# A new order of the ramp, with 60 matmuls on a zero tile, in a fused attention and gated-MLP kernel

## The chip, the cores and the metric

The kernel runs on one core of one Trainium2 chip. The metric is the device time of one execution in microseconds. Times are compared as medians of several runs. A profile comes from one further execution of the program.

## What is computed

The input is `q`, `k` and `v` with 4 batches, 8 heads, 768 positions and 64 columns. Heads 0, 2 and 6 ("retrieval") attend to all earlier positions; the other five ("streaming") attend to the first 4 positions and to a window of 64. The result of attention, 3072 rows of 512, goes through a gated layer of width 2048.

```
scores = scale * q @ k.T
mask   = causal                              # retrieval heads
mask   = causal & (is_sink | in_win)         # streaming heads, n_sink 4, window 64
a      = exp(scores - max) ; a = a / sum(a)
x      = a @ v                               # -> (B*S, H*D) = (3072, 512)
h      = x @ w_in                            # (3072, 2048)
g      = h * sigmoid(beta * h)
out    = g @ w_out                           # (3072, 512), float32
```

## The kernel before

The work is cut in eight chunks (a batch and a half of its 768 positions) and each chunk in four units (a pair of heads), 32 units in all. Each unit goes through the same steps:

- keys and queries arrive by DMA in float32 (tile `s`), are cast to bf16 (`qkb`, L246), transposed on TensorE (L322) and copied to the tiles `KT` and `QTD` (L330, L333). From unit 12 on, DMAs that cast and transpose do this instead (L282, L294, L297);
- values are cast to `VX` (L251); copies with the first four positions in front, for the streaming heads, go to `VO` (L259, L260) and `KO` (L312);
- scores go to a pair of PSUM banks (`sp`, L451). In the units up to 7 the masks are added first by a matmul with an identity (L422); later, and for unit 5, VectorE multiplies the exponentials by a mask (L478);
- ScalarE takes the exponential into `es` (L460), TensorE multiplies by the values into `po` (L520; odd units of the first eight use a bank of the pool `mm`), and VectorE divides (L529, L533) into `x`;
- `x` is transposed, on TensorE and by a copy in the first two chunks (L558, L567), by DMA later (L548), into `xT`.

The gated layer is cut in two kinds of steps: G1 makes 128 of the 2048 columns for a chunk (four matmuls of 128x384, L588), with a tanh on ScalarE (L593) and the gate on VectorE (L596); G2 adds four of sixteen products of 128x512 into an output tile (L641), which ScalarE scales (L645) and a DMA stores (L647).

The order of instructions on each engine is the order in which the program issues them; nothing reorders them afterwards. Up to unit 7 a string of words, `RAMP`, writes this order by hand: `ck`/`cq` cast keys or queries of a unit, `tk`/`tq` transpose them, `kk`/`kq` copy the transposes out (the last letter names the engine: v VectorE, a ScalarE, g GpSimd), `ko` copies sink keys, `ad`, `qk`, `ex` and `ma` are mask product, scores, exponential and mask multiplication of one score tile, `pv` is a third of a unit's value products, `no` its division, `xx` and `cx` the transposes of x and their copy, `lv`, `lq`, `wi`, `wo`, `ro` issue loads (a `g` at `lv` or `lq` lets a memset on GpSimd hold the load until that place in GpSimd's order), `cv`, `vo` and `on` prepare values, `mm` and `mA` issue a G1 step into a bank of one pool or the other, and `mb` a G2 step. `hm` and `hf` are the two halves of one G1 step. After that, `PLAN` does the same with one line per unit: `V` scores, `p` a sixth of the value products, `a`/`A` G1, `b` G2, `T` and `X` transposes.

Loads of keys, queries and values and the stores go through the queue of SP, two of the first loads through that of ScalarE, weights and later rows through that of GpSimd. `later` puts off some small VectorE and GpSimd steps by a planned delay.

Before the ramp, eight matmuls of 128x512 on a tile of zeros are issued (`idle(8, ps_m, "mm")`, L167, L168).

Of the kernel before, what the change touches and what calls it, by code (L numbers as in the profile page):

```python
# [10 lines left out]
F32 = mybir.dt.float32  # L11
# [7 lines left out]
def kernel(  # L19
# [13 lines left out]
    nc = tc.nc  # L33
# [348 lines left out]
    def steps_QK(u):  # L382
# [117 lines left out]
        some = 3 if len(tiles) == 3 else 2  # L500
        return [visit(range(i, min(i + some, len(tiles)))) for i in range(0, len(tiles), some)]

    def steps_PV(u):
        b, h2, p = units[u]
        s = st_u.setdefault(u, {})

        def head(hh, qi, last):
            def go():
                for f in s["masks"] + chunk_values[u // NPAIR] if u >= 8 else []:
                    f()  # L510
                if "po" not in s:
                    if u < 8 and u % 2:
                        po = ps_m.tile([128, 512], F32, name="mm")
                        s["po"] = po[:, 0:HT * 2 * (D + 1)].rearrange("p (t h d) -> p t h d", t=HT, h=2)
                    else:
                        s["po"] = ps_o.tile([128, HT, 2, D + 1], F32, name="po")
                po = s["po"]
                lst = s["blocks"][hh][qi]
                for j, (e, val) in enumerate(lst):
                    nc.tensor.matmul(po[:, qi, hh, :], e, val, start=(j == 0), stop=(j == len(lst) - 1))  # L520
# [142 lines left out]
    h = FO // 2  # L663
# [21 lines left out]
    def do(word):  # L685
# [7 lines left out]
        elif what in ("kk", "kq"):  # L693
            copy_qk(n, what[1], copies[eng])
        elif what == "ko":
            sinks_of(n)
        elif what in ("ad", "qk", "ex", "ma"):
            if n not in visits:
                visits[n] = steps_QK(n)
            step((0 if what in ("ex", "ma") else 170, lambda: visits[n][what](i)))  # L700
        elif what == "cv":
            cast_v(n, i, copies[eng])
        elif what == "vo":
            sink_values(n)
        elif what == "pv":
            pv = products.setdefault(n, [])
            if not pv:
                pv.extend(steps_PV(n))
            run(pv[:2])
            del pv[:2]  # L710
        elif what == "no":
            normalize(n)
        elif what == "xd":
            x_by_dma(n)
        elif what == "xx":
            run(steps_X(n))
        elif what == "cx":
            copy_x(n, copies[eng])
        elif what == "on":
            ones_v(engines[eng], n)  # L720
        elif what == "ne":
            negatives([(0, 1, 2), (3, 4)][n])
        elif what == "be":
            step((100, beta_go))
        elif what == "lv":
            load_v(n, held=eng == "g", tiles=[i])
        elif what == "lq":
            load_qk(n, i, held=eng == "g")
        elif what == "wi":
            load_w_in(n)  # L730
        elif what == "wo":
            load_w_out(n)
        elif what == "rq":
            rows_queries()
        elif what == "rk":
            rows_keys()
        elif what == "ro":
            if n not in more_rows:
                more_rows[n] = load_rows(n)
            more_rows[n].pop(0)()  # L740
        elif what in ("dk", "dq"):
            transposes_dma(n, what[1])
        elif what == "ml":
            late[n].pop(0)()
        elif what == "tt":
            run(steps_T(n))
        elif what == "hm":
            opened.append(done[0])
            done[0] += 1
            step(halves[0](opened[-1], 0))  # L750
        elif what == "hf":
            step(halves[0](opened.pop(0), 1))
        else:
            feed({"mm": "a", "mA": "A", "mb": "b"}[what])

    def feed(x):
# [24 lines left out]
        qk7.0 ad7.1 pv5 pv5 ex7.0 lv3.2 qk7.1 pv5 no5 ml1 wo1 ex7.1 pv6 pv6 wo2 mm pv7 rq  # L781
        pv7 pv7 no7 wo3 pv6 no6 rk cq8g xx2 ro3 cx2a mA mA ck8g xx3 cx3a mm mA
        mm mA mm mm mA mm mm mm mA mm ro3 mm mm mA mm mm mm ro3
        mA mm ro3 mA mm ro3 mm mm ro3 mA mA mb mb tt8 mb mb mb
    """
    words = RAMP.split()
    on_vector = {int(w[2]) for w in words if w.startswith("ma")}
    for word in words:
        do(word)

    PLAN = """
        ro3 ro3 ck9v b cq9a dk3 b cv2.1v cv2.0v vo2 T ro3 cv2.2v V cq11v a ro3 ro3 ro3 ck11a ro4 a b
        ck10a a dq3 a p cq10v a V p T p p p V p
        b T b p p p p p V p
        A b A a V ro4 p V a p p ro4 p p p
        ro4 V b p p p b p p ro4 p V b
        b p p p p X V p p a ro4 a ro4
        b A ro4 a a p V p ro4 p p ro4 b ro4 a a A ro4 A b b b dk4 A V a p dq4 p b A b
        p p p p p V p a a
        p p A p V p p p  # L800
        a a b b p p p p p p V a A A
        a b p p p p V p p
        b b a V p p p p p b a p
        b A A a a A p a A A a p b a p A p p p A A V b b b A
        p V p p p p p
        a A a b b p p p V p p b p a A
        a p A b p b p b A p b a p b p V A a
        V a p p b p p b V p p A
        b p p p p V p p
        A a b V b b a a p p b p A p a p a a A A p b V a b A b b  # L810
        p p p p V p p
        a A V b p A A p p p V p p a A
        a p b V b p p p p p
        V b a p a p p V A p A b b p p A A a
        p b V a p p p p A a p
        b a A p a p a a b a A p p A b a p b a p
        b A X a A b A
    """.strip().split("\n")
    TAIL = "aaAaA"

# [79 lines left out]
```

## Time and profile before

| what | value |
|---|---|
| median of 3 runs | 229.58 us (228.45 to 230.4) |
| the profiled execution's own time | 231.07 us |
| its span, first to last instruction | 229.1 us |
| TensorE (PE) busy | 223.1 us, 97% |
| ScalarE (ACT), VectorE (DVE), GpSimd (POOL) busy | 154.3, 141.8, 87.6 us |

The span is the time between the first and the last instruction of the program; the execution's own time is 1.97 us longer. The profile models the ends of matmuls, which are pipelined, so that a row of several matmuls gives their rate better than the duration of one. A row of the order of time reads: start, length, engine, line, operation, output<-inputs, shape, count, and in brackets the idle time before it with what ended it. A name with q (SPq) is the queue of an engine, in which DMAs are issued.

### The profile page before, as it was taken

How to read it: one execution, taken by the hardware profiler on the slowest of the kernel's cores; microseconds unless marked ns; L12 is line 12 of the kernel's file. 1: busy time of each engine (PE TensorE's matmuls, PEld its weight loads, DVE VectorE, ACT ScalarE, POOL GpSimd, SP SyncE). 2: the span in 40 equal slices, each digit the busy share in tenths (PEclk: the TensorE clock that was granted, in tenths of full speed). 3: DMA queues.
4: the chain of work that ended last, by engine and by line, in shares of the span. 5: the costliest groups of instructions: out<-in, count | busy, mean ns of one | idle time of the engine just before them, and what ended most of it. 6: DMA issues, size and time to landing. Idle time of an engine off the chain costs nothing.

```text
span 229.1 us, 5018 instructions
## 1 busy us (share of the span) xinstructions
PE 223.1 (97%) x1907; PEld 127.4 (56%) x1907; DVE 141.8 (62%) x342; ACT 154.3 (67%) x254; POOL 87.6 (38%) x143
## 2 busy tenths in 40 slices
PE   7899999999999999999999999999999999999994
PEld 2456666654565665555654565455654656455553
DVE  4458988875286588536952588546963779028600
ACT  2567988864868799438944697759876878138621
POOL 5373991219636269535028038940560000000000
PEclk9999999999999999999999999999999999999999
DMA  6999999999999999969778969496983130111012
GB/s 202 262 297 247 215 197 203 232 193 161 196 142 97 181 164 156 122 173 156 111 149 109 158 132 173 86 163 93 194 70 83 47 83 0 49 46 46 0 49 92
DMA packets 95383, 31.66 MB, mean 138 GB/s; under 512 B 81776, under 2 KB 92416, under 8 KB 95360
## 3 DMA queue, kind: packets, MB, share of 16 engines
q1 hardware_dynamic: 58880, 22.82, 48.6%
q0 software_dynamic: 35904, 8.13, 39.8%
q10 hardware_dynamic: 576, 0.40, 0.5%
q8 instruction: 15, 0.25, 0.4%
q14 instruction: 8, 0.07, 0.1%
HBM read 27.27 MB, written 6.29 MB: 146 GB/s over the span
## 4 chain that ended last, share of the span: by engine, by line
PE 94%; DMA 2%; ACT 1%; SPq 0%; issue 0%; ACTq 0%
PE mm L641 35%; PE mm L588 25%; PE sp L588 12%; PE sp L451 8%; PE po L520 7%; PE mm L322 2%; DMA s<-in_k_dram 2%; PE sp L422 2%; PE mm L626 2%; PE mm L558 1%; PE mm L520 1%; PE mm L451 1%; ACT qkb L246 1%; SPq L119 0%; ACT es L460 0%; ACT KT L330 0%
## 5 line engine op out<-in xcount | busy, mean ns | idle before, releaser
L641 PE MATMUL mm<-w_out_sb,gT 128*128 128x512 bf16 x368 | 85.9, 379 | 0.0
L460 ACT ACTIVATE es<-sp 128x768 bf16<-128x768 f32 (+2 forms) x72 | 56.6, 837 | 21.4 <-PE sp L451 21.2
L588 PE MATMUL mm<-xT,w_in_sb 128*128 128x384 bf16 x348 | 64.6, 326 | 0.0
L588 PEld LDWEIGHTS <-w_in_sb 128*128 128x128 bf16 x512 | 47.8, 98 | 29.8 <-issue 0.2
L593 ACT ACTIVATE th<-mm,beta_h 128x384 f32<-128x384 f32 x87 | 49.7, 587 | 5.7 <-PE mm L588 0.9
L641 PEld LDWEIGHTS <-gT 128*128 128x128 bf16 x368 | 33.4, 98 | 36.0 <-issue 1.5
L596 DVE SCALAR_TENSOR_TENSOR gT<-th,mm 128x384 bf16<-128x384 f32 x87 | 46.7, 551 | 6.7 <-ACT th L593 3.2
L282 POOL DMA_DIRECT2D s<-in_q_dram x30 | 22.4, 763 | 26.3 <-DMA QTD<-s 19.8
L588 PE MATMUL sp<-xT,w_in_sb 128*128 128x384 bf16 x164 | 32.3, 326 | 0.0
L645 ACT ACTIVATE osb<-mm 128x512 f32<-128x512 f32 x23 | 13.9, 603 | 25.5 <-PE mm L641 25.2
L520 PEld LDWEIGHTS <-es 128*128 128x128 bf16 x472 | 23.8, 99 | 12.8 <-issue 1.5
L596 DVE SCALAR_TENSOR_TENSOR gT<-th,sp 128x384 bf16<-128x384 f32 x41 | 22.3, 552 | 5.6 <-ACT th L593 3.7
L282 POOL DMA_DIRECT2D s<-in_k_dram x30 | 22.4, 760 | 8.5 <-DMA w_out_sb<-in_moe_w_out_dram 5.8
L593 ACT ACTIVATE th<-sp,beta_h 128x384 f32<-128x384 f32 x41 | 23.7, 585 | 2.3 <-PE sp L588 0.2
L520 PE MATMUL po<-VX,es 128*128 128x65 bf16 x360 | 25.2, 195 | 0.0
L251 POOL CAST VX<-vs 128x512 bf16<-128x512 f32 x16 | 10.1, 632 | 36.4 <-DMA vs<-in_v_dram 30.2
L529 DVE RECIPROCAL rec<-po 128x6 f32<-128x6 f32 x28 | 5.4, 193 | 29.1 <-PE po L520 29.1
L451 PE MATMUL sp<-QTD,KT 64*128 64x128 bf16 (+2 forms) x258 | 20.1, 249 | 0.6 <-ACT QTD L333 0.4
L478 DVE TENSOR_TENSOR es<-es,Mh 128x768 bf16<-128x768 bf16 (+1 forms) x26 | 15.5, 626 | 5.0 <-ACT es L460 4.4
L533 DVE TENSOR_TENSOR x<-po,rec 128x384 bf16<-128x384 f32 x28 | 15.6, 557 | 1.0
L451 PEld LDWEIGHTS <-KT 64*128 64x128 bf16 x278 | 11.4, 96 | 6.2 <-issue 3.9
L259 POOL COPY VO<-VX 128x512 bf16<-128x512 bf16 x16 | 10.8, 696 | 6.2 <-DVE VX L251 6.2
(72 smaller groups left out, 160.3 us busy)
## 6 DMA issues: line engine op xcount, KB each, us to landing
vs<-in_v_dram SPq DMA_DIRECT2D x24, 256.0 KB, 5.2
out_dram<-osb SPq DMA_DIRECT2D x23, 256.0 KB, 2.6
w_in_sb<-in_moe_w_in_dram POOLq DMA_DIRECT2D x4, 512.0 KB, 9.3
w_out_sb<-in_moe_w_out_dram POOLq DMA_DIRECT2D x4, 512.0 KB, 16.8
s<-in_k_dram POOLq DMA_DIRECT2D x30, 64.0 KB, 4.8
s<-in_q_dram POOLq DMA_DIRECT2D x30, 64.0 KB, 4.9
s<-in_k_dram SPq DMA_DIRECT2D x4, 384.0 KB, 6.8
s<-in_q_dram SPq DMA_DIRECT2D x4, 384.0 KB, 6.5
```

The costliest lines, as they stand in the source:

```text
L259: copy(out=vo[:, i - 1, :, 0:D], in_=vx[:, i, :, 0:D])
L282: nc.gpsimd.dma_start(out=ROWS[c % 2, name][:, t, i * 4 * D:(i + 1) * 4 * D].rearrange("p (h d) -> p h d", d=D), in_=src[b, i:H:2, r:r + 1 ...
L451: nc.tensor.matmul(sps[i][r][:, x * 128:y * 128], key(a, lhs), s["QT"][half(a), qi * 128:(qi + y - x) * 128], start=first, stop=first or y ...
L460: nc.scalar.activation(out=views[i].rearrange("p r k j -> p r (k j)"), in_=banks[2][:, :, 0:n * 128], func=ACTF.Exp, scale=scale)
L478: nc.vector.tensor_mul(ev[:, :, 0:n], ev[:, :, 0:n], Mh[h2][:, None, m0:m0 + n].to_broadcast([128, 2, n, 128]))
L520: nc.tensor.matmul(po[:, qi, hh, :], e, val, start=(j == 0), stop=(j == len(lst) - 1))
L533: nc.vector.tensor_mul(xg[g][:, :, :, u % 2, :].rearrange("p a t d -> p t a d"), po[:, :, :, 0:D], rec.to_broadcast([128, HT, 2, D]))
L588: nc.tensor.matmul(hp[:, 0:HALF], w_in_sb[:, mo, fi * 128:(fi + 1) * 128], xT[c][:, mo, :], start=(mo == 0), stop=(mo == MO - 1))
L593: nc.scalar.activation(out=th, in_=hp[:, 0:HALF], func=ACTF.Tanh, scale=beta_h[:, fi:fi + 1])
L596: nc.vector.scalar_tensor_tensor(out=gTs[c][:, fi, :], in0=th, scalar=1.0, in1=hp[:, 0:HALF], op0=ALU.add, op1=ALU.mult)
L641: nc.tensor.matmul(op, gTs[c][:, fi, ns * 128:(ns + 1) * 128], w_out_sb[:, fi, :], start=(fi == 0), stop=(fi == FO - 1))
L645: nc.scalar.activation(out=osb, in_=op, func=ACTF.Copy, scale=0.5)
```

## The change

A word `zz10` in `RAMP` issues ten matmuls of a 128x128 tile of zeros with 122 columns of zeros (`keep_busy`). They write the last 122 columns of the PSUM bank in which unit 0 gathers its value products; these columns are never read. The bank is made by `sums_bank`, so that it exists before unit 0's first product. `zz10` stands six times in the ramp: once before and once after the transposes `tq0`, then after `tq1`, after `tk1`, after the scores of unit 0 and before those of unit 1.

The rest of the ramp keeps its steps, and many change place or engine. The query cast of unit 0 goes from VectorE to ScalarE, the copies of its transposes change sides, the key copies of units 0, 1 and 3 go from VectorE to ScalarE, two value casts come to VectorE, one copy of xT goes from VectorE to ScalarE, and the half steps `hm` and `hf` become one whole step. `PLAN` keeps nearly all of its steps, with others as neighbours; its G1 and G2 steps stand at other places among the attention steps, and the casts of units 10 and 11 change engines. Besides the 60 matmuls and their weight loads, TensorE has the same number of instructions as before.

```diff
+    banks_o = {}
+
+    def sums_bank(u):
+        if u not in banks_o:
+            banks_o[u] = ps_o.tile([128, 512], F32, name="po")
+        return banks_o[u]
+
+    def keep_busy(n):
+
+        z = HT * 2 * (D + 1)
+        for i in range(n):
+            nc.tensor.matmul(sums_bank(0)[:, z:512], zeros[:, 0:128], zeros[:, 0:512 - z], start=True, stop=True)
...
-                        s["po"] = ps_o.tile([128, HT, 2, D + 1], F32, name="po")
+                        s["po"] = sums_bank(u)[:, 0:HT * 2 * (D + 1)].rearrange("p (t h d) -> p t h d", t=HT, h=2)
...
+        elif what == "zz":
+            keep_busy(n)
...
     RAMP = """
-        ck0g ne1 lv0.0 lv0.1 tk0 ck2a ne0 cq0v ck1a tq0 kq0a ad0.0 on0v lv0.2 kk0v cq1v tq1 qk0.0
-        tk2 ad0.1 kq1v tk1 kk1v lq1.0g be qk0.1 ex0.0 ad1.0 cv0.0g ko1 lq1.1 ex0.1 pv0 ck3v cq3g tk3
-        lv1.0g cq2a tq2 kk3v lv1.1 cv0.1g ad1.1 qk1.1 kk2v ex1.1 tq3 ko2 qk1.0 wi0 vo0 cq4g lv1.2 cv0.2a
-        lq2.0g ko3 pv0 kq2v pv0 ad2.0 qk2.0 lv2.0 ex1.0 pv1 kq3a pv1 ck4v ad2.1 qk2.1 lv2.1 pv1 ex2.0
-        ad3.0 tq4 no0 tk4 ex2.1 ck7g kk4a qk3.0 ad3.1 qk3.1 no1 pv2 ck6v ex3.0 cq5v ck5g pv2 tk6
-        xx0 ad4.0 cq6g pv3 kq4v ex3.1 pv2 ad4.1 cx0v ad5.0 qk4.1 pv3 lv2.2 no2 on1g tq5 pv3 qk4.0
-        kk6a ml0 tk5 cq7g kq5v ex4.1 kk5a ko5 ko6 ad5.1 tq6 wi1 qk5.0 ex4.0 tk7 tq7 ex5.0 no3
-        qk5.1 ex5.1 kq6v xx1 ad6.0 kk7v wi2 kq7v wi3 cx1a qk6.0 ml1 ad6.1 ex6.0 cv1.1g ko7 qk6.1 cv1.0v
-        ex6.1 hm lq2.1 ma5.0 ma5.1 mm cv1.2g vo1 mm wo0 pv4 lv3.0g ad7.0 lv3.1 pv4 hf pv4 no4
...
+        ck0g cq0a lv0.0g cq1g ck2a zz10 on0g ne0 ne1 tq0 zz10 ad0.0 lv0.1 ad0.1 tk0 lv0.2 tq1 zz10 ck1v kq0v tk1 kk0a
+        zz10 qk0.1 qk0.0 lq1.0 zz10 ad1.0 lq1.1 cq3g kk1a ck3a cv0.0v be ad1.1 ex0.0 ex0.1 tk3 ko1 cq2a tq2 kq1v kk3a
+        tk2 kk2v pv0 zz10 qk1.1 ex1.1 ko3 qk1.0 lv1.0 lv1.1 tq3 cv0.1g ko2 wi0 pv0 lv1.2 vo0 cq4g ad2.0 cv0.2v lq2.0g
+        ex1.0 kq2v qk2.0 pv1 ad2.1 ck4v kq3a pv0 pv1 lv2.0g ex2.0 ck7g qk2.1 ex2.1 pv1 ad3.0 tq4 tk4 kk4a qk3.0 ad3.1
+        lv2.1 lv2.2 no0 no1 pv2 qk3.1 ck6v kq4v ex3.0 ex3.1 xx0 cq5v pv2 ck5g tk6 pv3 ad4.0 ad4.1 pv2 cx0a ad5.0 kk6a
+        cq6v pv3 qk4.0 qk4.1 on1g ad5.1 pv3 tq5 tk5 ex4.1 no2 tq6 kq5v cq7g kk5a ko5 ko6 qk5.0 ex4.0 tk7 no3 tq7 ex5.0
+        qk5.1 kq6v wi1 ml0 xx1 ma5.0 ex5.1 wi2 ml1 ad6.0 wi3 lq2.1g qk6.0 cx1a ex6.0 ad6.1 qk6.1 kk7v ex6.1 cv1.1g mm
+        ko7 ma5.1 cv1.2g cv1.0v vo1 mm pv4 kq7v ad7.0 mm pv4 lv3.0 pv4 lv3.1 wo0 pv5 ad7.1 lv3.2 no4 qk7.0 qk7.1 pv5
...
     PLAN = """
-        ro3 ro3 ck9v b cq9a dk3 b cv2.1v cv2.0v vo2 T ro3 cv2.2v V cq11v a ro3 ro3 ro3 ck11a ro4 a b
-        ck10a a dq3 a p cq10v a V p T p p p V p
...
+        ck9v ro3 cv2.1v cq9a ro3 b a cv2.0v T vo2 ro3 cq10a cv2.2v V dk3 ck10v ro3 cq11v a ck11v ro3 ro3 a A ro4
+        dq3 a T b b ro4 p p p p V p p V
...
```

More of the change, by code (lines that the diff above doesn't have):

```diff
@@ L785 @@
+        xx3 cx3a mm ro3 mA mm mA ro3 mm mm mm mA mm ro3 mm mA mm mm mm mA ro3 mm mA mm mm mA mA mm mm mm mA mA mb mb
+        mb tt8 mb mb
     """
@@ L791 @@
     PLAN = """
-        ro3 ro3 ck9v b cq9a dk3 b cv2.1v cv2.0v vo2 T ro3 cv2.2v V cq11v a ro3 ro3 ro3 ck11a ro4 a b
-        ck10a a dq3 a p cq10v a V p T p p p V p
[L794 to L810, printed above, removed]
-        p p p p V p p
[L812 to L817, printed above, removed]
+        ck9v ro3 cv2.1v cq9a ro3 b a cv2.0v T vo2 ro3 cq10a cv2.2v V dk3 ck10v ro3 cq11v a ck11v ro3 ro3 a A ro4
+        dq3 a T b b ro4 p p p p V p p V
+        A T ro4 a p p p p p A V p
+        a b a V A V p ro4 p p p p p
+        V A b p p p p V p p
+        A A V p X p p p p p b A ro4
+        ro4 A b a p ro4 V p p ro4 ro4 ro4 p a a ro4 b A A b ro4 b dk4 p b V dq4 p A b b b
+        a A V p p p p p p b b
+        p p V A p p p p
+        b b a p p V a p p p p b A b
+        b p p p b p p p V
+        a a a p V p p p p p b
+        b A A a a a p A a a p b p A p p b p A V b A
+        V p b p b a p b a A p p b p
+        A A b p b p a p V b p p a p
+        b A A b p p p p p b b A a A A p V A
+        b V p p p p A a p p V b a
+        p p p p p p V
+        a A V b p b b p a p p A a A a p p A b A V b a A b a b
+        p p p p V p p
+        a b b p p V A a b p p p V p A a a
+        p p V A p p p p A
+        V p b p p a p b b A V p p a a b A b a
+        V a p p p p p A A b a a p A a b
+        a p p a p A p p p a A
+        a a X A a b
     """.strip().split("\n")
```

5 lines of the change are left out of this document (1 added, 4 removed).

## The prediction

> **What bounds the kernel now.** I read the page's engine line first, then the busy time by stretches, then the order of time on each engine in the first 32 us.
>
> ```profile
> span 229.1 us, 5018 instructions
> PE 223.1 (97%) x1907; PEld 127.4 (56%) x1907; DVE 141.8 (62%) x342; ACT 154.3 (67%) x254; POOL 87.6 (38%) x143
> ...
> 5.00:10.00 5.00, 3.91 (x31) 2.36 (x30) 2.82 (x9) 2.11 (x4) 0.60 (x2) 1.00 1.23 273
> 10.00:15.00 5.00, 4.88 (x40) 2.41 (x41) 3.26 (x8) 3.39 (x6) 3.98 (x10) 1.00 1.10 305
> 15.00:20.00 5.00, 5.00 (x70) 3.27 (x68) 2.73 (x7) 3.67 (x6) 2.62 (x10) 1.00 1.24 234
> ...
> 30.00:220.00 190.00, 190.00 (x1576) 107.40 (x1573) 120.98 (x293) 133.60 (x219) 69.01 (x95) 1.00 0.89 124
> 220.00:229.10 9.10, 5.84 (x59) 4.29 (x57) 0.29 (x1) 1.26 (x3) 0.00 (x0) 1.00 0.25 88
> ```
>
> In a stretch's row the columns are its length, then busy time of PE, PEld, DVE, ACT and POOL with counts, then the granted clock. From 30 to 220 us PE is busy 190.00 of 190. So a new order there can gain next to nothing; it can only add a wait. What can be won lies ahead of 30 us. The whole ramp up to there reads like this on PE:
>
> ```profile
> 1.29 3.59 PE L167 MATMUL mm<-zeros 128*128 128x512 bf16 x8 [1.29 <-DVE zeros L157]
> ...
> 5.51 0.50 PE L322 MATMUL mm<-idb,qkb 128*128 128x128 bf16 x3 [0.17 <-DVE qkb L246]
> ...
> 6.71 0.50 PE L322 MATMUL mm<-idb,qkb 128*128 128x128 bf16 x3 [0.48 <-DVE qkb L246]
> 7.64 0.51 PE L451 MATMUL sp<-QTD,KT 64*128 64x128 bf16 x4 [0.43 <-ACT QTD L333]
> ...
> 16.48 0.83 PE L422 MATMUL sp<-Ns,idb 128*128 128x384 bf16 x2
> ...
> 18.70 0.33 PE L322 MATMUL mm<-idb,qkb 128*128 128x128 bf16 x3
> ...
> 24.41 1.80 PE L588 MATMUL mm<-xT,w_in_sb 128*128 128x384 bf16 x10
> ...
> 26.11 0.49 PE L422 MATMUL sp<-Ns,idb 128*128 128x384 bf16 x2
> ...
> 31.41 0.51 PE L558 MATMUL mm<-idb,x 128*128 128x128 bf16 x6
> ```
>
> The same work is slow first and fast later: three 128x128 transposes take 0.50 us at 6.71 and 0.33 at 18.70; two 128x384 mask products take 0.83 at 16.48 and 0.49 at 26.11. The difference is 0.17/3 = 57 ns for 128 columns and 0.17 us for 384, so TensorE streams at half rate up to a point between 16.5 and 18.7 us, 17.3 by the single instructions, and at full rate after it. The clock column says 1.00 from the first stretch on; the durations contradict it, and I go by them.
>
> **The price of the slow clock.** Groups of PE from 7.2 to 17.3 us, shapes apart:
>
> ```profile
> L322 PE MATMUL mm<-idb,qkb 128*128 128x128 bf16 x18 | 3.3, 309 | 0.1
> L451 PE MATMUL sp<-QTD,KT 64*128 64x128 bf16 x19 | 2.4, 302 | 0.4 <-ACT QTD L333 0.4
> L422 PE MATMUL sp<-Ns,idb 128*128 128x384 bf16 x5 | 2.2, 514 | 0.0
> L451 PE MATMUL sp<-QTD,KT 64*128 64x256 bf16 x6 | 1.3, 403 | 0.0
> L520 PE MATMUL po<-VX,es 128*128 128x65 bf16 x12 | 1.1, 243 | 0.0
> L422 PE MATMUL sp<-Nc,idb 128*128 128x256 bf16 x3 | 1.1, 420 | 0.0
> L422 PE MATMUL sp<-Ns,idb 128*128 128x256 bf16 x3 | 1.0, 415 | 0.0
> ```
>
> By column I take 0.44 ns saved at full clock (57 ns / 128; 0.17 us / 384). Transposes: 18 x 56 ns = 1.0. QK products go in pairs (two 64-row halves together): 10 pairs of 128 = 0.6, 3 pairs of 256 = 0.35. Masks: 5 x 170 = 0.85 and 6 x 113 = 0.7. PV products, 65 columns: 12 x 28 = 0.35. Together 3.8 us, if the clock rises at 7.2 instead of 17.3.
>
> **The zero matmuls.** Each has 122 columns. By the eight of L167 (3.59 us for 8 x 512, less 0.2 us of drain: 0.83 ns a column) one costs 102 ns at half clock and about 51 at full: a lot of ten is 1.0 or 0.5 us. Lots stand before the first q transposes (`tq0`), before the masks of unit 0, after `tq1`, after `tk1`, after unit 0's QK and before unit 1's. The PE waits of before that could swallow them up to the first QK are 0.17 + 0.48 + 0.43 = 1.1 us; the lots up to there are four. With the clock up at 7.2, two lots at half rate and four at full come to 4.1 us, 3.0 of them on top of the waits. So on PE alone the change is worth 3.8 - 3.0 = 0.8 us. If the clock stayed down, all six would cost 6.1.
>
> When does the clock rise? Lot 1 follows the eight at 4.7 us without a gap, `tq0` follows at 5.7, lot 2, masks, `tk0`, `tq1` and lot 3 up to 8.3: PE streams from 1.3 to 9 us without a hole. Before, PE was busy 3.91 of 5 us from 5 to 10, 4.88 from 10 to 15 and only then 5.00 of 5; there the clock rose. I take 7.2, between 4.7 and 8.1.
>
> The Trainium skill, TensorE: Matmul & The Clock Gate, section "What's actually happening", says that the array runs at half clock after idling and at full clock after one busy window of some 3.4 us, and that this window runs freely, not from the kernel's start. The rise at 17.3 fits it; that eight zero matmuls of 3.59 us did not raise it fits only if the window lay across them. Its note that the warm-up is under 1% of a typical span speaks against a large gain; the 3.8 us above are 1.7%.
>
> **What the other engines allow.** PE is not alone on this path. ACT and DVE:
>
> ```profile
> 8.18 0.81 ACT L460 ACTIVATE es<-sp 128x768 bf16<-128x768 f32 x1 [0.59 <-PE sp L451]
> ...
> 12.58 0.60 ACT L460 ACTIVATE es<-sp 128x512 bf16<-128x512 f32 x1 [1.35 <-PE sp L451]
> ...
> 21.66 2.01 ACT L460 ACTIVATE es<-sp 128x768 bf16<-128x768 f32 x3
> ...
> 25.60 1.23 ACT L593 ACTIVATE th<-mm,beta_h 128x384 f32<-128x384 f32 x2
> ```
>
> ```profile
> 24.02 0.75 DVE L251 CAST VX<-vs 128x512 bf16<-128x512 f32 x1
> 24.69 1.94 DVE L478 TENSOR_TENSOR es<-es,Mh 128x768 bf16<-128x768 bf16 x2
> ...
> 30.79 0.56 DVE L533 TENSOR_TENSOR x<-po,rec 128x384 bf16<-128x384 f32 x1
> 31.27 0.54 DVE L596 SCALAR_TENSOR_TENSOR gT<-th,mm 128x384 bf16<-128x384 f32 x1
> 33.26 0.56 DVE L596 SCALAR_TENSOR_TENSOR gT<-th,mm 128x384 bf16<-128x384 f32 x1 [0.53 <-ACT th L593]
> ```
>
> I walked the new order through these durations. Four lots stand ahead of unit 0's QK, which comes at 9.0 instead of 7.64; the first exponential starts at 9.6, not 8.18. From there ACT has eleven exponentials of 0.70 and three of 0.50 (three take 2.01 in the row at 21.66), six casts or copies of 0.45 and two copies of xT of 0.75 (`cx0` came over from DVE): 13.4 us, so no earlier than 23.0. My walk finds 1.6 us of waits in it (PE's masks wait for score banks, unit 1's PV for the sink values, below), so ACT is free for the first gate at 24.6 instead of 25.60: 1.0 gained. The first product with w_in comes at 23.3 instead of 24.41: 1.1.
>
> POOL delays something:
>
> ```profile
> 9.40 0.61 POOL L251 CAST VX<-vs 128x512 bf16<-128x512 f32 x1 [4.55 <-DMA vs<-in_v_dram]
> ...
> 12.53 0.87 POOL L140 DMA_DIRECT2D w_in_sb<-in_moe_w_in_dram  x1
> 13.40 0.62 POOL L259 COPY VO<-VX 128x512 bf16<-128x512 bf16 x1
> 14.08 0.61 POOL L260 COPY VO<-VX 4x512 bf16<-4x512 bf16 x1
> ```
>
> Unit 3's key copy now stands ahead of a value cast on POOL and waits for ACT's `kk3a`; behind it come that cast, `ko2`, the first w_in load and the sink values, ready at 15.5 instead of 14.7. The load itself starts 0.9 later.
>
> Then DVE sets the pace, as it does now: from 24.02 to 31.35 it never idles, and the second transposition of x (31.41 on PE) waits for its last product. In the new order it starts its masks of unit 5 at 22.0 instead of 24.69, as soon as ACT has that exponential; but the value cast (0.7), a key copy, a query copy (0.5 each) and a mask copy (0.6) now come after that point. 22.0 + 6.7 (24.69 to 31.35) + 2.3 - 0.1 = 30.9: 0.4 gained where DVE decides. The queries and keys cast on ACT instead of DVE, and `on0` on POOL, are in that walk and cost nothing by themselves.
>
> **Edits of the later order.** The half product `hm`/`hf` becomes a whole one; casts of units 10 and 11 change between ACT and DVE; row loads of k and q and VO copies swap on POOL; some loads of v go before or behind output stores on SP; products of G1 and G2 move by one or two places between the attention steps. All keep the number of instructions and DMAs. PE's 190.00 of 190 hides them as long as no operand is late; one that is late by a step costs at most a part of G2, four products of 128x512, 0.86 us. A cap on the gain, not a loss, is the load of w_out:
>
> ```profile
> 28.50 2.23 POOL L144 DMA_DIRECT2D w_out_sb<-in_moe_w_out_dram  x3
> ...
> DMA to landing us min/median/max: 11.9/16.8/21.2
> ...
> 50.71 2.54 PE L641 MATMUL mm<-w_out_sb,gT 128*128 128x512 bf16 x11
> ```
>
> The last of the four is issued at 29.96 and lands up to 21.2 later, at 51.2; its first reader is the fourth part, which starts at 50.71 + 0.86 = 51.6. So PE may come 0.4 us earlier for nothing, more only if these loads are issued earlier. In the new order three stand directly behind the sink values and the fourth behind two casts; POOL reaches them some 2 us sooner by my walk, so I count no wait.
>
> **Sum.** Between the places where ACT and PE gain 1.0 to 1.1 and the place where DVE gains 0.4; PE alone gives 0.8. I take 0.9, since the value 0.4 rests on four DVE pieces of which the last two need not precede unit 4's products. Span 229.1 - 0.9 = 228.2; the profiled execution of before took 231.07, 1.97 more than its span, so its counterpart would take 230.2. The median shown is 229.58, 1.5 below that execution; I subtract from the median: 228.7 us.
>
> **Rivals.**
> A, the whole prize. If ACT and DVE keep up with a full-rate PE, the 3.8 us come in, and the four full-rate lots (2.0) fall into waits of PE; only 4.1 - 1.1 - 2.0 = 1.0 of the zeros is left. 3.8 - 1.0 = 2.8 us: 226.8. For it: DVE idles and ACT waits for PE in the ramp (1.35 at 12.58). Against: DVE from 24 to 31 is full.
> B, the lots don't raise the clock. It is slower than before: 6.1 us of zeros on PE between 4.7 and 13, of which the waits of before cover at most 2.5 (1.1, and 1.35 at 12.58): +3.6, 233.2. For it: 3.59 us of zero matmuls did not raise it at 4.9. Against: the later rise followed dense work, and there will be 7 us of it. It decides if the transposes at 8 us still take 0.50 for three.
> C, the clock is already up early in many executions of before (times shown run from 228.45 to 230.4, more than a saturated PE explains). Then the 3.8 us are not there to win, and four lots at full rate beyond the waits, with two at half, cost 3.0: 232.6. It decides by how early the transposes of the before kernel quicken in other executions. The skill's free-running window, of the page named above, would make this happen by chance of phase.
> D, the early clock with a late operand after 30 us: two waits of a G2 part, 1.7 us, cancel the gain: 230.4, within 1%.
>
> **Chances.** My forecast 0.37, with D 0.04: within 1% 0.41. A 0.36: faster by over 1%. B 0.12 and C 0.11: slower by over 1%, 0.23. (1%, 2.3 us, is about what a measurement of this kernel can tell from no change.) The range takes in all of the forecast and D, A (226.8, and 0.8 below it for a PE that waits still less) and part of C: 226.0 to 232.0. The likeliest case's own range is 227.5 to 229.8, from 2.1 gained (if DVE's pieces fall into gaps) to 0.2 lost (clock up at 8.1 only).
>
> **What would show it.** Three transposes 0.33 us long by 8.5 us; first exponential between 9 and 10; first product with w_in near 23.3; the second transposition of x near 31.0, with DVE full before it; PE 190 of 190 afterwards. It is wrong if three transposes still take 0.50 after 9 us, if the second transposition is earlier than 29.5, or if PE shows idle time between 35 and 220.

## The result, and the profile after

The changed kernel takes 231.45 us (median of 22 runs, 229.57 to 232.25); before takes 229.57 (22 runs of the same session, 228.03 to 231.62). The ratio is 1.0084, with a 95% interval of 1.006 to 1.0107. So the change costs 1.9 us, where 0.9 were to be gained. A ratio leaves out executions over 1.5% above the fastest of their kernel, so it can differ a little from that of the medians given. The profiled execution of after takes 231.87 us with a span of 229.8.

The profile's engine line and three stretches of after, with the same columns as in the prediction:

```profile
span 229.8 us, 5122 instructions
...
PE 220.7 (96%) x1948; PEld 129.6 (56%) x1967; DVE 140.6 (61%) x339; ACT 156.0 (68%) x256; POOL 86.5 (38%) x144
```

```profile
5.00:10.00 5.00, 4.75 (x75) 4.35 (x74) 1.68 (x5) 2.73 (x6) 1.70 (x5) 1.00 1.22 273
10.00:15.00 5.00, 4.70 (x67) 3.33 (x67) 3.15 (x8) 3.93 (x8) 3.10 (x6) 1.00 1.11 310
...
30.00:220.00 190.00, 188.43 (x1552) 107.17 (x1570) 120.34 (x292) 133.93 (x218) 66.78 (x93) 1.00 0.93 124
```

There are 1948 matmuls but 1967 weight loads: 19 matmul records are missing, 18 of them in the long stretch, and they look like idle time. Order of time on PE in the ramp of after:

```profile
4.68 1.23 PE L514 MATMUL po<-zeros 128*128 128x122 bf16 x10
5.70 0.51 PE L322 MATMUL mm<-idb,qkb 128*128 128x128 bf16 x3
...
7.81 0.33 PE L322 MATMUL mm<-idb,qkb 128*128 128x128 bf16 x3
7.97 0.70 PE L514 MATMUL po<-zeros 128*128 128x122 bf16 x10
8.60 0.51 PE L451 MATMUL sp<-QTD,KT 64*128 64x128 bf16 x10
...
23.00 1.47 PE L601 MATMUL mm<-xT,w_in_sb 128*128 128x384 bf16 x8
25.70 0.22 PE L533 MATMUL po<-VX,es 128*128 128x65 bf16 x2 [1.23 <-DVE VX L251]
...
31.12 0.51 PE L571 MATMUL mm<-idb,x 128*128 128x128 bf16 x6
...
222.40 3.70 PE L639 MATMUL mm<-w_out_sb,gT 128*128 128x256 bf16 x48
```

The clock rises near 6.1 us: three transposes take 0.51 at 5.70 and 0.33 at 7.81. In this execution the walk of the prediction comes out nearly to the point: scores 8.60 (9.0 said), first product with w_in 23.00 (23.3), second transposition of x 31.12 (31.0; 31.41 before). But then PE waits 1.23 us for a value cast, and 0.3 us of lead at 31 us are no lead at the end. The last matmuls end at 222.40 + 3.70 = 226.10, that is 194.98 after the second transposition; before it was 194.44 (222.15 + 3.70 - 31.41):

```profile
222.15 3.70 PE L626 MATMUL mm<-w_out_sb,gT 128*128 128x256 bf16 x48
```

From there to the span's end after needs 3.7 us, before 3.3. So this execution is behind by 0.7: 0.3 gained in the ramp, 0.5 and 0.4 lost later.

### The profile page after: what moved, and what is told of

Same layout as the page of the kernel before. It is cut to its first block, busy times and chain, and to the rows that moved or that the text cites. A ratio compares the mean times of both kernels' runs of the same rounds, so it can differ in the third digit from the quotient of the medians.

```text
span 229.8 us, 5122 instructions
## 1 busy us (share of the span) xinstructions
PE 220.7 (96%) x1948; PEld 129.6 (56%) x1967; DVE 140.6 (61%) x339; ACT 156.0 (68%) x256; POOL 86.5 (38%) x144
## 4 chain that ended last, share of the span: by engine, by line
PE 87%; DVE 3%; DMA 2%; issue 2%; ACT 2%; POOL 2%; POOLq 0%; ACTq 0%
PE mm L654 32%; PE mm L601 24%; PE sp L601 12%; PE po L533 6%; PE sp L451 6%; DMA xT<-x 2%; PE mm L167 2%; PE mm L639 2%; ACT es L460 1%; PE mm L322 1%; DVE es L478 1%; PE po L514 1%; PE sp L422 1%; PE mm L571 1%; PE mm L451 1%
## 5 line engine op out<-in xcount | busy, mean ns | idle before, releaser
L654 PE MATMUL mm<-w_out_sb,gT 128*128 128x512 bf16 x349 | 84.7, 379 | 1.3 <-issue 0.5
L460 ACT ACTIVATE es<-sp 128x768 bf16<-128x768 f32 (+2 forms) x72 | 56.4, 839 | 13.4 <-PE sp L451 13.0
L609 DVE SCALAR_TENSOR_TENSOR gT<-th,mm 128x384 bf16<-128x384 f32 x86 | 46.6, 552 | 15.5 <-ACT th L606 11.1
L606 ACT ACTIVATE th<-mm,beta_h 128x384 f32<-128x384 f32 x86 | 49.2, 590 | 8.6 <-PE mm L601 4.8
L533 PEld LDWEIGHTS <-es 128*128 128x128 bf16 x472 | 22.7, 97 | 13.6 <-issue 2.6
L282 POOL DMA_DIRECT2D s<-in_q_dram x30 | 22.5, 769 | 16.7 <-DMA QTD<-s 10.8
L606 ACT ACTIVATE th<-sp,beta_h 128x384 f32<-128x384 f32 x42 | 24.4, 585 | 4.1 <-PE sp L601 1.6
L533 PE MATMUL po<-VX,es 128*128 128x65 bf16 x360 | 23.9, 194 | 1.2 <-DVE VX L251 1.2
L251 POOL CAST VX<-vs 128x512 bf16<-128x512 f32 x15 | 9.5, 636 | 40.1 <-DMA vs<-in_v_dram 30.2
L609 DVE SCALAR_TENSOR_TENSOR gT<-th,sp 128x384 bf16<-128x384 f32 x42 | 22.9, 553 | 2.8 <-ACT th L606 0.4
L451 PE MATMUL sp<-QTD,KT 64*128 64x128 bf16 (+2 forms) x258 | 18.6, 240 | 0.0
L259 POOL COPY VO<-VX 128x512 bf16<-128x512 bf16 x16 | 9.7, 629 | 6.7 <-DVE VX L251 6.7
```

Of the source, the lines that this page charges most:

```text
L259: copy(out=vo[:, i - 1, :, 0:D], in_=vx[:, i, :, 0:D])
L282: nc.gpsimd.dma_start(out=ROWS[c % 2, name][:, t, i * 4 * D:(i + 1) * 4 * D].rearrange("p (h d) -> p h d", d=D), in_=src[b, i:H:2, r:r + 1 ...
L451: nc.tensor.matmul(sps[i][r][:, x * 128:y * 128], key(a, lhs), s["QT"][half(a), qi * 128:(qi + y - x) * 128], start=first, stop=first or y ...
L460: nc.scalar.activation(out=views[i].rearrange("p r k j -> p r (k j)"), in_=banks[2][:, :, 0:n * 128], func=ACTF.Exp, scale=scale)
L606: nc.scalar.activation(out=th, in_=hp[:, 0:HALF], func=ACTF.Tanh, scale=beta_h[:, fi:fi + 1])
L609: nc.vector.scalar_tensor_tensor(out=gTs[c][:, fi, :], in0=th, scalar=1.0, in1=hp[:, 0:HALF], op0=ALU.add, op1=ALU.mult)
```

## The experiments

Before is not one execution. Of 121 timed executions of it beside these kernels half took under 229.3 us, and only 16 took 231.07 or more, as the profiled one did. Each ratio below is to runs of before on the same chip.

| kernel | ratio to before | 95% interval |
|---|---|---|
| after, again (e11) | 1.0076 | 1.004 to 1.0112 |
| new ramp alone (e10) | 0.9992 | 0.9955 to 1.0028 |
| new PLAN alone (e9) | 1.0019 | 0.9984 to 1.0053 |
| 60 zero matmuls alone (e3) | 1.0051 | 1.0028 to 1.0074 |
| new ramp, new PLAN (e2) | 1.0031 | 0.9994 to 1.0069 |
| new ramp, 60 zeros (e7) | 1.0038 | 1.001 to 1.0066 |
| after, wide zeros (e12) | 1.0016 | 0.9977 to 1.0056 |
| before, wide zeros (e13) | 1.0015 | 0.9982 to 1.0047 |
| before, 14 zeros (e4) | 0.9992 | 0.9965 to 1.0018 |

From the profile of each: when the clock rose (clock record of the trace), when the first 16 KB packet of the instruction queue q8 started, when the key load issued near 9.6 us landed, when the second transposition of x began, and how long it took from there to the last matmul's end and on to the span's end. In e2 and e10 the clock fell in between.

| kernel | clock up | packet | key load | x | to last | to end |
|---|---|---|---|---|---|---|
| before | 17.4 | 18.7 | 15.4 | 31.41 | 194.44 | 3.3 |
| after | 6.1 | 13.4 | 16.1 | 31.12 | 194.98 | 3.7 |
| e11 | 4.5 | 12.1 | 16.6 | 30.14 | 194.57 | 3.7 |
| e7 | 4.4 | 12.0 | 16.5 | 30.00 | 194.39 | 3.3 |
| e3 | 5.1 | 12.2 | 16.9 | 31.97 | 194.45 | 3.3 |
| e6 | 7.2 | 14.0 | 16.4 | 31.42 | 194.66 | 3.7 |
| e12 | 4.2 | 15.3 | 15.5 | 28.88 | 194.76 | 3.7 |
| e13 | 7.0 | 16.0 | 15.3 | 30.45 | 194.39 | 3.3 |
| e4 | 6.1 | 16.6 | 15.2 | 28.93 | 194.39 | 3.3 |
| e14 | 6.6 | 16.3 | 15.1 | 30.31 | 194.38 | 3.3 |
| e2 | 6.4, again 13.3 | 18.3 | 15.9 | 30.36 | 194.75 | 3.7 |
| e10 | 5.2, again 12.0 | 17.1 | 15.2 | 28.87 | 194.44 | 3.3 |
| e9 | 10.6 | 18.0 | 15.2 | 29.06 | 194.75 | 3.7 |
| e5 | 10.9 | 18.5 | 16.9 | 30.66 | 194.38 | 4.7 |

### Was there a slow clock to win back?

e1 is before, unchanged.

> The kernel before, unchanged, for a second profile. Theory P (phase): whether the TensorE clock rises early in the ramp is a matter of chance in this kernel; the execution profiled first was a late one (three transposes 0.50 us long up to 17.3 us, 231.07 us), most others rise by about 5 to 6 us. So this profile shows either early transposes of 0.33 us by 8 us and a time of 228.0 to 229.5, or 0.50 us up to 14 to 18 us and 230 to 231.6. Theory O (order): the clock rises at 17.3 us in every execution, whatever the time; the loss of the change sits in the new order after 31 us.

It took 231.07 us, clock up at 17.4, second transposition at 31.37: nearly the same trace as the first. Both profiles show a late clock, so these two alone tell nothing of the timed executions.

e4 adds 14 zero matmuls to before, as many as fit into PE's waits:

```diff
-... cq0v ck1a tq0 kq0a ad0.0 on0v lv0.2 kk0v cq1v tq1 qk0.0
+... cq0v ck1a zz3 tq0 kq0a ad0.0 on0v lv0.2 kk0v cq1v zz6 tq1 zz5 qk0.0
```

> The kernel before with 3, 6 and 5 zero matmuls (102 ns each at half clock) ahead of its first q transposes, of unit 1's q transposes and of the first score product, where it waits 0.36, 0.67 and 0.59 us, and no others. Theory P: the clock is up by 8 us in nearly every execution and nothing is delayed: 228.0 to 228.9, faster than before by 0.3 to 0.7%, with less spread. Theory O: as before, 229.2 to 229.9.

Median 228.38. Its profiled span, 226.6, is 2.5 below that of before, yet its times are no better than before's on that chip (0.9992), where the expectation had 0.3 to 0.7% of gain. So most executions of before can't be as late as the profiled one. e5 takes the eight zero matmuls out instead:

```diff
-    idle(8, ps_m, "mm")
```

> The kernel before without its eight zero matmuls of 128x512 at the start. Theory P: these eight raise the clock early in most timed executions of before; without them nearly every execution is a late one, like the profiled one of before: a median of 230.3 to 231.5, 1.5 to 2.5 over before, and three transposes still 0.50 us long at 10 us. Theory O: they do nothing (the profile shows the clock down until 17.3 us with them): within 0.4 of before.

Median 230.81, ratio 1.0081 (1.0047 to 1.0115). That is the time that theory P named, but the profile of e5 doesn't show a late clock as the cause: it rises at 10.9, while a key load lands at 16.9 and the end takes 4.7 us. The mean granted clock of the timed executions tells more. In 59 of the 121 executions of before it is 0.993 or less, in all others 0.997 or more. The traces of e10 (mean 0.992) and e2 (0.991) show what that means: the clock was up early and fell back for a step of 3.4 us. None of e5's twelve executions has such a mean, and none of the 34 of after and e11. So in about half of the executions of before the eight matmuls raise the clock early, and it doesn't always stay up. An early rise turned up in the profile of e9, whose ramp is that of before, unchanged. PE of e9:

```profile
9.65 0.82 PE L422 MATMUL sp<-Ns,idb 128*128 128x384 bf16 x2
...
11.73 0.34 PE L322 MATMUL mm<-idb,qkb 128*128 128x128 bf16 x3
...
22.26 1.80 PE L588 MATMUL mm<-xT,w_in_sb 128*128 128x384 bf16 x10
...
29.06 0.50 PE L558 MATMUL mm<-idb,x 128*128 128x128 bf16 x6
```

The same instructions as in before, with the rise at 10.6 instead of 17.4: the second transposition comes at 29.06, not 31.41. That is 2.35 us that need no change of the kernel. An earlier rise adds little to it: e4, e8, e10 and e12, with the clock up (in e10 for good) at 6.1, 6.2, 12.0 and 4.2, have the transposition at 28.84 to 28.93. So the condition of rival C holds; its price of 3.0 us for the lots is another matter (below). What decides between 10.6 and 17.4 is open. The two rises lie two steps of 3.41 us apart, so the steps lie at the same place in both executions; in the step from 7.17 to 10.58 PE was busy 2.98 us in before and 3.25 in e9, but 3.30 us in before's next step did not raise the clock either.

### The three parts one by one

e2 is after without the six lots:

```diff
-... ck2a zz10 on0g ne0 ne1 tq0 zz10 ad0.0 ...
+... ck2a on0g ne0 ne1 tq0 ad0.0 ...
```

> The changed kernel with all six lots of zero matmuls left out, its order kept. Theory P: the zeros cost about what they keep TensorE from (some 2 us up to the first score product), and without them the clock rises early only by chance: a median of 229.5 to 231.0 with a spread of 2 us or more, not slower than the changed kernel. Theory O: the new order alone is the loss: 231 or more, within 0.5 of the changed kernel.

Median 230.32, ratio 1.0031: over half of the loss goes with the lots, which theory O does not allow. e3 is before with the six lots of ten at the corresponding places:

```diff
-... ck1a tq0 kq0a ... tq1 qk0.0 / ... tk1 kk1v ... qk0.1 ex0.0 ... ad1.1 qk1.1 ...
+... ck1a zz10 tq0 zz10 kq0a ... tq1 zz10 qk0.0 / ... tk1 zz10 kk1v ... qk0.1 zz10 ex0.0 ... ad1.1 zz10 qk1.1 ...
```

> The kernel before with the six lots of ten zero matmuls at the corresponding places of its own order. Theory P: the zeros alone make the change's loss: 230.5 to 232, with a clock that is up by 8 us in every execution. Theory O: no slower than before, 228.5 to 229.8.

Median 229.77, below what theory P said and yet 0.5% over before on that chip, so the lots alone make a part of the loss, not the whole. In its profile PE waits 1.39 us for the second part of w_in, but that execution, 231.53, is the second slowest of twelve. e7 is after with the old later order:

```diff
-    PLAN = """ ck9v ro3 cv2.1v cq9a ...
+    PLAN = """ ro3 ro3 ck9v b cq9a ...
```

> The changed kernel's ramp with zeros, and the later order (PLAN) of the kernel before. Theory P: the later order loses at most 0.6 us (PE from the second transposition of x to its end: 194.97 against 194.44 us in the profiles): a median 0.3 to 1.0 below the changed kernel. Theory O: the whole loss is in the later order: the median falls by 1.5 to 2, to that of before.

Median 230.17, 1.3 below after: between the two theories. e9 is before with only the new `PLAN`, e10 before with only the new order of the ramp (no lots, old `PLAN`); e11 is after once more.

> The kernel before with only PLAN, the later order, taken from the changed kernel; ramp and zeros as before. Theory L (the later order costs time wherever it stands, some 0.55 us between 30 us and the last matmul and 0.43 us after it): 0.8 to 1.4 us slower than before on the same chip, from the last matmul to the span's end 3.7 us. Rival M (the later order is only dear behind the new ramp, because the ramp leaves the engines in another phase): within 0.4 us of before, and 3.3 us at the end.

> The kernel before with only the ramp's order taken from the changed kernel: no zero matmuls and the old PLAN. If the parts add (zeros 1.1, later order 1.3, as the runs with one of them taken from the changed kernel gave, and 1.9 in all), the ramp's order alone is 0.5 us faster than before, between -1.0 and 0. If the parts don't add, because the new order has the clock rise late more often without the zeros, it is 0.3 or more slower than before, in two groups of times.

> The changed kernel once more, for a second profile of it and more times on this chip. Its times fell in two groups so far, about 229.6 to 230.1 and 231.2 to 232.3. If the groups come from where the clock rises (before or after the transposes of unit 0), this profile agrees with the first when its own time does (231.9, second transposition of x at 31.1), and has that transposition at 30.1 or earlier when its own time is near 230. If they come from something after 30 us, the transposition is at 31.1 either way.

Medians 229.91, 229.92 and 231.44. By its time e9 lies with rival M (ratio 1.0019, not to be told from 1), by its end of 3.7 us with theory L. The parts add: with and without the lots the ratios differ by 0.0051 (e3), 0.0046 (e7 less e10), 0.0045 to 0.0053 (after or e11, less e2); with and without the new PLAN by 0.0019 (e9), 0.0039 (e2 less e10), 0.0038 to 0.0046. That is about 1.1 us for the lots and 0.8 for the later order, each with some 0.8 of uncertainty where single ratios are subtracted; the order of the ramp alone is worth nothing that can be told from zero.

The later order is seen in the traces too. In the six profiles with the new PLAN (after, e2, e6, e9, e11, e12) the last matmul ends 194.57 to 194.98 us after the second transposition, and the span 3.7 later; in the ten with the old one (e1 and e8 among them) it is 194.38 to 194.48, and 3.3 in all but e5 (4.7, behind a late store). PE of e9 ends at 220.11 + 3.70, of e10 at 219.61 + 3.70:

```profile
span 227.5 us, 5023 instructions
```

```profile
220.11 3.70 PE L626 MATMUL mm<-w_out_sb,gT 128*128 128x256 bf16 x48
```

```profile
span 226.6 us, 5015 instructions
```

```profile
219.61 3.70 PE L639 MATMUL mm<-w_out_sb,gT 128*128 128x256 bf16 x48
```

227.5 - 223.8 = 3.7, and 226.6 - 223.3 = 3.3. The records of SyncE in the traces show where these 0.4 us lie. Its closing drain starts 0.35 to 0.36 us after its last wait for a semaphore and takes 0.12 to 0.13 in all six profiles with the new PLAN; in the ten with the old one it starts after 0.05 and takes 0.01. SyncE has 212 instructions with the new PLAN and 210 with the old; whether that is the reason is not shown. Part of the rest is a late operand: of PE's waits in after from 31.5 to 226 us (us in total, times, longest) one is for a mask product,

```profile
PE po L533 <- DVE es L478: 0.2, 1, 0.2
```

and e9 and e12 have the same, e2 one of 0.3; before has none there, nor have e6 and e11, which with 194.66 and 194.57 are the shortest of the six. e11's case of two groups of times: its profiled execution, 230.51, has the clock up at 4.5 and the transposition at 30.14, against 231.87, 6.1 and 31.12 of the first. So in these two profiles the ramp makes 1.0 of the 1.4 us of difference, on the side of the first of the two expectations; the twelve times of e11 (229.91 to 232.2) don't fall in two groups, so more than that is not shown.

### Why do the zeros cost time?

e6 was aimed at PE's wait of 1.23 us. In after, VectorE's value cast and POOL run like this:

```profile
23.35 0.74 DVE L478 TENSOR_TENSOR es<-es,Mh 128x512 bf16<-128x512 bf16 x1
24.02 1.64 DVE L251 CAST VX<-vs 128x512 bf16<-128x512 f32 x1
```

```profile
23.71 0.53 POOL L312 COPY KO<-KT 128x128 bf16<-128x128 bf16 x1
24.20 0.61 POOL L251 CAST VX<-vs 128x512 bf16<-128x512 f32 x1
24.76 0.61 POOL L259 COPY VO<-VX 128x512 bf16<-128x512 bf16 x1
```

The cast that took 0.75 before takes 1.64 beside POOL's casts and copies, and ends 0.3 after the last of the three. In e4 it comes at 21.07, while POOL only issues DMAs, and takes 0.49:

```profile
21.07 0.49 DVE L251 CAST VX<-vs 128x512 bf16<-128x512 f32 x1
21.48 0.87 DVE L478 TENSOR_TENSOR es<-es,Mh 128x768 bf16<-128x768 bf16 x2
```

The Trainium skill, SBUF — State Buffer, section "SBUF: two separate sides", says that VectorE and GpSimd share one pair of ports, that an instruction which uses the pair holds it to its end, and that the other side blocks meanwhile. The 0.49 against 1.64 agree with that, if this cast is one that uses the pair. e6 moves the cast ahead of unit 5's masks:

```diff
-... qk5.1 kq6v wi1 ml0 xx1 ... cv1.2g cv1.0v vo1 ...
+... qk5.1 kq6v cv1.0v wi1 ml0 xx1 ... cv1.2g vo1 ...
```

> The changed kernel with one step moved: the VectorE cast of the first value tile of chunk 1 goes back ahead of the mask products of unit 5. Theory P with the order's own loss in this place: the wait of 1.23 us before unit 4's value products goes, the second transposition of x comes 0.6 to 1.0 earlier than in the changed kernel (31.1), the median falls by 0.6 to 1.2, to 230.3 to 230.9. A theory that the loss sits in the zeros or in the later order alone: no change, 231.2 to 231.7.

It missed: 231.17, ratio 1.0071 (1.0039 to 1.0104). The clash only moves to the mask product that now stands there, and PE waits 1.08 us:

```profile
21.74 0.66 DVE L251 CAST VX<-vs 128x512 bf16<-128x512 f32 x1
...
23.98 1.98 DVE L478 TENSOR_TENSOR es<-es,Mh 128x512 bf16<-128x512 bf16 x1
```

The second profile of after (e11) shows another loss. Its clock is early and its first exponential 0.75 ahead of the first profile's, but at the first product with w_in (23.35 against 23.00) it is behind:

```profile
7.06 0.33 PE L322 MATMUL mm<-idb,qkb 128*128 128x128 bf16 x3
...
14.67 0.49 PE L422 MATMUL sp<-Ns,idb 128*128 128x384 bf16 x2
16.10 0.51 PE L322 MATMUL mm<-idb,qkb 128*128 128x128 bf16 x6 [0.95 <-POOL s L115]
...
23.35 1.47 PE L601 MATMUL mm<-xT,w_in_sb 128*128 128x384 bf16 x8
```

```profile
15.54 0.51 POOL L246 CAST qkb<-s 128x384 bf16<-128x384 f32 x1 [1.04 <-DMA s<-in_q_dram]
```

PE waits for a query cast, and POOL's cast for its load. e7 has the same wait of PE, 0.84. The first profile of after has it not: there the packet starts at 13.4 and that load lands at 14.0, in e11 at 15.4. One thing stands in this load's way that does not in before: the packet of instructions. The DMA queues (packets, MB, share of 16 engines) of e11 from 12 to 13 us, of before from 18 to 19:

```profile
q1 hardware_dynamic: 416, 0.31, 104.8%
q8 instruction: 1, 0.02, 7.1%
```

```profile
q8 instruction: 1, 0.02, 5.8%
```

7.1% of 16 engines is one engine for 1.14 us. The packet comes the earlier the more matmuls were issued: at 17.1 to 18.7 us with none added, 16.3 to 16.8 with 14, 12.0 to 14.0 with 60. There it lies ahead of the key and query loads, which land at 15.1 to 15.4 and 16.4 to 16.7 in seven of the other profiles (e2 and e5 are later). To test it, e12 (on after) and e13 (on e3) issue the same zero columns of the first five lots in 15 matmuls instead of 50; the sixth lot comes behind unit 0's first value product and stays as it was:

```diff
-        for i in range(n):
-            nc.tensor.matmul(sums_bank(0)[:, z:512], zeros[:, 0:128], zeros[:, 0:512 - z], start=True, stop=True)
+        if "po" in st_u.get(0, {}):
+            for i in range(n):
+                nc.tensor.matmul(sums_bank(0)[:, z:512], zeros[:, 0:128], zeros[:, 0:512 - z], start=True, stop=True)
+        else:
+            left = n * (512 - z)
+            while left > 0:
+                w = min(left, 512)
+                nc.tensor.matmul(sums_bank(0)[:, 0:w], zeros[:, 0:128], zeros[:, 0:w], start=True, stop=True)
+                left -= w
```

> The changed kernel with the same number of zero columns in the first five lots, but in 15 matmuls (512, 512 and 196 columns a lot) instead of 50; the sixth lot keeps its ten. TensorE streams as long as before and the clock rises as early. Theory F (the 70 instructions more, each matmul with its weight load, bring TensorE's 16 KB packet of instructions at 12 to 14 us instead of 17 to 19, in front of the key and query loads that the ramp waits for, and it holds one DMA engine for 1.0 to 1.3 us): the packet comes at 15 us or later, the key load issued at about 9.6 lands at 15.2 instead of 16.1 to 16.6, the second transposition of x comes near 29.3, and the median falls by 0.8 to 1.2 us against the changed kernel's 231.44. Rival Z (the zeros cost their time on TensorE): nothing of the sort moves, and the median stays within 0.3 of 231.44.

> The order of before with the six lots, the first five in 15 wide matmuls of the same columns. With 60 narrow ones the packet of instructions came at 12.2, the key load landed at 16.9, and the ratio to before was 1.0051. Theory F: packet at 15 us or later, key load at 15.3, ratio 0.996 to 1.000, near that of the 14 zero matmuls. Rival Z: ratio 1.003 to 1.007 as with 60.

e12 takes 230.28 us. PE streams the same zeros (a lot takes 0.68 instead of 0.70), but the packet comes at 15.3, the key load lands at 15.5, PE waits for neither it nor the cast (0.84 here), and the ramp is 1.1 us ahead of e11 at w_in and 1.26 at the second transposition of x:

```profile
4.45 0.68 PE L520 MATMUL po<-zeros 128*128 128x512 bf16 x3
...
8.18 0.69 PE L520 MATMUL po<-zeros 128*128 128x512 bf16 x3
...
28.88 0.51 PE L578 MATMUL mm<-idb,x 128*128 128x128 bf16 x6
```

So in these two executions, both with the clock up before the lots, the time of the zeros on PE is free; what costs is their number. The medians agree (231.44 to 230.28); the interval of e12's ratio, up to 1.0056, overlaps that of e11 (from 1.004) and not that of after's first measurement (from 1.006).

It isn't the whole price. In the first profile of after PE waits for no load. Its first lot runs ahead of the rise of the clock and takes 1.23 us instead of 0.70; its first exponential comes at 9.15, against 8.40 in e11 and 8.29 in e12, before any late load matters. And in the order of before the wide zeros bring nothing: e13 takes 229.83 us, e3 with narrow ones 229.77. In ratios (1.0015 and 1.0051) the intervals overlap and leave both theories open. Both are far above e4 and e8, 228.38 and 228.33, with 14 zeros. The loads of e13 land like those of e4, yet its ramp is 1.4 us later at the first transposition of x and 1.5 at the second. PE of e4, then of e13:

```profile
7.36 0.34 PE L451 MATMUL sp<-QTD,KT 64*128 64x128 bf16 x4
8.73 0.50 PE L422 MATMUL sp<-Ns,idb 128*128 128x384 bf16 x2
...
16.27 0.50 PE L571 MATMUL mm<-idb,x 128*128 128x128 bf16 x6
```

```profile
8.16 0.34 PE L451 MATMUL sp<-QTD,KT 64*128 64x128 bf16 x4
...
10.57 0.49 PE L422 MATMUL sp<-Ns,idb 128*128 128x384 bf16 x2
...
17.65 0.50 PE L578 MATMUL mm<-idb,x 128*128 128x128 bf16 x6
```

There it is the columns on PE that cost, some of them at half clock (the clock rose at 7.0 in e13, at 6.1 in e4); e3, with the clock up at 5.1, has its first transposition of x as late, at 17.84. How much of the 1.1 us is columns and how much late loads in the median execution of after is not shown.

e8 (the second w_in load earlier, on top of e4) and e14 (14 zeros in the new order, old PLAN) look for a better version. The lines of e8 are against e4, those of e14 against e10:

```diff
-... cq7g kq5v ... tq6 wi1 qk5.0 ...        # e8
+... cq7g wi1 kq5v ... tq6 qk5.0 ...
-... ck2a on0g ne0 ne1 tq0 ad0.0 ... tq1 ck1v ...        # e14
+... ck2a zz3 on0g ne0 ne1 tq0 zz6 ad0.0 ... tq1 zz5 ck1v ...
```

> The kernel before with 3, 6 and 5 zero matmuls in its first waits, as in the earlier run, and the second load of w_in issued ahead of two sink key copies on GpSimd instead of behind them. If the landing of that load caps what an early clock gives: its first reader, the fifth G1 product, no longer waits and the median falls to 227.2 to 228.2, with the executions near 229.6 gone. If it does not: 228.2 to 228.6 as without the move.

> The new order of the ramp with the old PLAN, and 14 zero matmuls (3, 6 and 5) where the first three lots of the change stand. The new ramp's order alone gave a ratio of 0.9992 in several groups of times, with the clock up, down and up again. If the order is worth something once the clock stays up and the loads land at 15.2, the ratio is 0.992 to 0.996 and the second transposition of x comes before 28.8. If the landing of the loads is the floor of either order, the transposition comes at 28.8 to 29.1 and the ratio is 0.996 to 1.000, as with the 14 in the old order.

e8: 228.33, ratio 0.9961 (0.9932 to 0.9989), the only kernel below 1 by its interval. The expectation without an effect of the move (228.2 to 228.6) is the one that fits. Its load lands 1.8 us earlier than e4's (25.77 against 27.57), which nothing waits for: the profiled spans are 226.5 and 226.6, so the gain is that of e4, on a chip where before was slower. e14: 229.31, 0.9997 (0.9959 to 1.0036), with the transposition at 30.31, later than either theory had it. Its key load lands at 15.1, but the cast takes 1.64 again and PE waits:

```profile
22.21 1.47 PE L601 MATMUL mm<-xT,w_in_sb 128*128 128x384 bf16 x8
24.92 0.22 PE L533 MATMUL po<-VX,es 128*128 128x65 bf16 x2 [1.24 <-DVE VX L251]
```

In the new order this cast follows the masks directly and meets POOL's casts in after, e2, e7, e11 and e14 (1.08 to 1.64; 0.84 in e10 and e12); in the old order it takes 0.49 to 0.85.

## Why the prediction was wrong

- "I subtract from the median" is the step that failed first. The 3.8 us of slow clock belong to the profiled execution; in the same ramp with the rise at 10.6 (e9) 2.35 of it are gone, and half of before's executions take under 229.3. Rival C, with a chance of 0.11, had the condition right: the 0.9 gained was not there to be won. Its 232.6 came from 3.0 us for the lots, and they cost 1.1.
- Of the edits of the later order the prediction said that PE's 190.00 of 190 hides them. That was wrong by about 0.8: 0.1 to 0.6 between the second transposition and the last matmul, 0.4 after it. The view with PE at 190.00 of 190 can't show either: the same share of busy time holds a stretch that is 0.3 longer, and the end lies outside it. Rival D is in it on a small scale, one operand late by 0.2 us, where it counted 1.7.
- "Two lots at half rate and four at full come to 4.1 us, 3.0 of them on top of the waits" was set against a saving of 3.8, and so the lots came out as a gain on PE. They cost about 1.1 net: the saving was there only in late executions, and the price was smaller than 3.0 and of two kinds. As columns they cost nothing where the clock was up before them (e12), and about 1.5 in the order of before (e13 against e4 and e8). As 60 instructions they make the loads late (e11), which no step of the prediction looked at: it costed the loads of w_in and w_out, not those of keys and queries.
- Right: the lots keep the clock up. In the ten profiles with zeros added (14 or more) it is up for good from 4.2 to 7.2; in the six without, from 10.6 to 17.4. So B is out. Near, too, were scores, first exponential (9.15, 9.6 said), w_in and second transposition in the profiled execution. That the last one fits to 0.1 is luck: the second profile of the same kernel has 30.14. The value 0.4 rested on four DVE pieces of the trace's lengths; one of them, the value cast, took 1.64 instead of 0.75, and PE waited 1.23 us for it, a wait that the walk did not have.
- A did not happen even where ACT and DVE kept up (e12, with waits of PE of at most 0.5 us in the ramp from 9 us on): it takes 230.28, as the new PLAN costs and before has an early clock of its own.

The sum now: 0.9 not to be had, 1.1 for the lots, 0.8 for the later order make 2.8 us; 231.45 - 228.7 is 2.75. With some 0.8 us of uncertainty in the parts, and parts taken in part from the same runs, so close an agreement shows little.

Open: why SyncE's closing drain comes 0.4 later with the new PLAN; how the 1.1 us of the lots divide between columns and late loads; whether the packet explains the loads in every execution (in e5 the key load lands at 16.9 with the packet at 18.5; the cause of that is not known).

## What to carry to other kernels

Ask of a profiled execution where it lies among the timed ones before costing what it shows; a prize that half of the executions have already isn't one. Add no more filler work than fits into the waits: 14 zero matmuls cost nothing here, 60 cost 1.1 us. It can be paid in instructions as well as in time, so look at what it does to the packets of instructions and to the loads behind them. An engine at 190 of 190 shows that nothing waits there, not that the work behind that stretch stays as long.

## What the hardware showed that was not expected

- The packet of instructions: 16 KB, 0.93 to 1.30 us on one DMA engine. The key load issued near 9.6 us takes 6.4 to 7.1 us to land in the five profiles with 60 narrow zeros, where the packet starts ahead of its landing at 12.0 to 14.0 us, and 5.5 to 5.8 in nine of the ten where the packet starts after it (7.2 in e5). In e12, where it starts 0.2 us before the landing, it is 6.2.
- The clock fell again. PE of e10, which has only the eight zero matmuls, up near 5.2, down at 8.6, up at 12.0:

```profile
5.50 0.33 PE L322 MATMUL mm<-idb,qkb 128*128 128x128 bf16 x3
...
8.61 0.80 PE L422 MATMUL sp<-Ns,idb 128*128 128x384 bf16 x2 [1.03 <-ACT es L460]
...
12.25 0.32 PE L422 MATMUL sp<-Ns,idb 128*128 128x384 bf16 x1
```

  Between 5.5 and 8.6 PE waited three times, 1.03 us before the last. e2, without zeros too, does the same: up at 6.4, down at 9.9, up at 13.3. The steps are 3.4 us apart; the Trainium skill, TensorE: Matmul & The Clock Gate, section "What's actually happening", gives the free-running window as 3.4 us, and the trace agrees. The clock column of the stretches said 1.00 throughout in before, as the trace's record of the clock begins only at its first rise, at 17.43 there; 0.99 is the run's mean in e10.
- VectorE's cast of 128x512 took 0.49 to 1.64 us, by what POOL did beside it.
